# New ranks, fewer q loads and row-wise v tails in a pooled-attention and gated-convolution kernel

## The chip, the core and the metric

The kernel runs on one core of a Trainium2 chip. A core has a matrix engine (TensorE, PE in the profile, with its weight loads as PEld), a vector engine (VectorE, DVE), an activation engine (ScalarE, ACT), a general engine (GpSimd, POOL) and a small engine that here only issues transfers (SyncE, SP). Each engine runs its own instructions in the order in which they were written; semaphores order the engines against each other. Transfers run on 16 DMA engines. The metric is the time of one execution on the device in microseconds (us), as the median of several runs.

## The reference

Eight batches, eight heads, 576 positions, head size 64. Keys and values are averaged over groups of 8 positions, so 576 queries see 72 keys in each head. The attention output, 576 x 512 per batch, goes through a gated feed-forward part:

```
k_p = k.reshape(B, H, 72, 8, D).mean(axis=3);  v_p likewise
attn = softmax(q @ k_p^T / sqrt(D))            # 576 x 72 in each head
x = (attn @ v_p), heads side by side           # 576 x 512 in each batch
h = relu(x @ w_in)                             # 576 x 1024
conv = sum over 3 taps of conv_w[k] * h shifted by k - 1
out = (h * sigmoid(conv)) @ w_out              # 576 x 512
```

All inputs and the output are float32; the kernel computes in bf16 and accumulates in float32.

## The kernel before

**Work by batch.** k, v and q are loaded batch by batch by transfers issued from POOL, which turn float32 into bf16 on the way. Each batch has two buffers in turn (`k_b`, `v_b`, `q_b`, `q2`, `qT`, `attnT`, `xT`, `hT`). VectorE sums 8 neighbours of k (steps kp1, kp2 and ksum, L590, L597 and L607) and of v (vp1, vp2, va, L639), TensorE transposes the sums of k (kT, L620), and these are copied into `kz` (L627). The sums of v are multiplied by a mask into block form (`vblk`, L643 and L648).

v is cut into tiles of 128 rows (L462) and a fifth tile, the tail. The tail holds, for each of four pairs of heads, 32 rows around the 16 that the other tiles lack. One transfer brings all 128 rows (L467); the mask drops what is not wanted.

q comes in two ways. For batches 0 to 4 a transfer of 64 rows and one of 8 (L419) fill `q_b`, a copy regroups it (qg, L427), TensorE transposes it (qT, L673), and copies bring it to `qT` (qTe, L679). For batches 5 to 7 five transfers (L407) bring q by rows of positions, and five crossbar transposes issued from SP (qD, L661) turn it into `qT`, one for each 128 positions. In those batches the attention output is transposed in the same way (xD, L757); in the others by TensorE and a copy (xt and xte, L764 and L770).

Then come the scores (sc, L702 and L704, five steps to a batch; in batches 5 to 7 each reads all five tiles of `qT`), their exponentials on ScalarE (L710), the product with `vblk` (av, L727 and L731), the normalization on VectorE (rc and nm, L740 and L744), the transposes, and the first product (mm1, L784 in batch 0, L807 in the others, eight steps of eight matmuls) with its relu on ScalarE (L813). The convolution is done for a few feature blocks on TensorE (L930, with diagonal weights that POOL builds at L559), for the others by two scalings (cp, L853 on ScalarE or L855 on VectorE) and two sums (L862, L872). The gate follows (L880 or L937 on ScalarE, L908 and L918 on VectorE). The second product (mm2, L961) is done for pairs of batches, in nine tiles of 128 rows; a copy (oe, L984) and a store from SP (st, L989) end it.

**Order.** The program does not write its steps in the order of this list. Each step is first added to a planner with its engine, a duration, what it reads and writes, and, for transfers, their load on the DMA engines. The planner goes through a model of the engines' time: at each point it takes, for each engine, the steps that could start first, and among those that could start within 0.02 us of each other the one with the lowest rank. The ranks are the list `prio`, one whole number for each step in the order in which steps are added. What the planner picks is the order in which the instructions are written, so on the chip each engine has that order and waits where an input is late. The list `act` names the steps that go to ScalarE where both ScalarE and VectorE could do them (cp, oe, qTe, qg, xte, kz); the others go to VectorE. Where the model shows TensorE idle in the first 60 us, `warm` puts in matmuls of zeros (L383).

The transfers issued from POOL use eight semaphores in turn, so the ninth waits for the first to land. The names below have the batch behind the first point: `ldq5.2` is the third load of q of batch 5, `mm2.1.0.0` the first tile of pair 1 in the second product.

Of the kernel before, what the change touches and what calls it, by code (L numbers as in the profile page):

```python
# [61 lines left out]
    "act": (  # L62
# [38 lines left out]


TINY = 1e-20


class Op:
    __slots__ = ("i", "name", "eng", "dur", "lat", "deps", "prio", "fn", "take", "give", "dma", "done", "users", "after", "kind", "unit", "mode")


class Planner:  # L110

# [973 lines left out]
```

## Time and profile before

| | |
|---|---|
| median of 3 runs | 213.72 us (212.86 to 215.43) |
| the profiled execution itself | 213.99 us |
| its span, first to last instruction | 212.3 us |
| busy PE, DVE, ACT, POOL | 196.0, 171.6, 163.6, 57.5 us |
| mean granted TensorE clock | 0.980 |
| read from HBM, written | 33.57 MB, 9.44 MB |

Busy times are those of the span. The page of the profile gives them by engine and in slices of the span; other views group instructions by line, list them in order of time, follow the chain of work that ended last, or name who waited for whom. A row in order of time has its start and its duration in us, the engine, the line, what is written and read, the number of instructions put together, and in brackets the idle time of the engine just before it with what ended that time. In a row that groups instructions by line, behind "x" and their number stand busy us and mean ns of one, then the idle time before them.

### The profile page before, as it was taken

The page shows a single profiled execution, that of the slowest core. Times are in us where ns is not written, and L with a number is a line of the kernel's source. Part 1 is how long each engine was busy: PE and PEld are TensorE (multiplying, and loading weights), DVE is VectorE, ACT ScalarE, POOL GpSimd, SP SyncE. Part 2 cuts the span into 40 slices and gives each one's busy share as a digit, 9 for nine tenths or more (in the row PEclk, how much of TensorE's full clock was granted, in tenths as well). Part 3 has the DMA queues.
Part 4 walks back from the last instruction along what each step waited for, and adds up shares of the span by engine and source line. Part 5 has one row for each costly group of instructions (what it writes and reads, how often), then busy time and mean ns, then how long its engine had stood idle before and what let it go on. Part 6 is the DMA issues. An engine that isn't in the chain of part 4 may idle for free.

```text
span 212.3 us, 4596 instructions
## 1 busy us (share of the span) xinstructions
PE 196.0 (92%) x1776; PEld 133.6 (63%) x1792; DVE 171.6 (81%) x395; ACT 163.6 (77%) x275; POOL 57.5 (27%) x91
## 2 busy tenths in 40 slices
PE   8999988989999959993799999999999999999993
PEld 8988665857576627761376668655755864675541
DVE  3578499999999778999079999997999999478620
ACT  2025599999999947994479999999998995998512
POOL 7993598443241357334400000000000000000000
PEclk9999999999999999999589999999999999999998
DMA  4999999999999999999999117424523503600434
GB/s 67 186 191 201 175 204 194 185 203 180 196 167 244 235 181 148 157 116 152 181 178 126 76 69 139 106 57 131 148 49 114 148 0 84 208 21 0 170 131 148
DMA packets 52282, 30.08 MB, mean 142 GB/s; under 512 B 33356, under 2 KB 47268, under 8 KB 52260
## 3 DMA queue, kind: packets, MB, share of 16 engines
q0 software_dynamic: 32336, 16.79, 67.9%
q1 hardware_dynamic: 19924, 12.99, 24.8%
q8 instruction: 14, 0.23, 0.5%
q14 instruction: 8, 0.07, 0.1%
HBM read 33.57 MB, written 9.44 MB: 203 GB/s over the span
## 4 chain that ended last, share of the span: by engine, by line
PE 52%; DMA 28%; DVE 7%; POOL 5%; SPq 4%; issue 2%; ACT 0%; ACTq 0%; DVEq 0%; POOLq 0%
PE psfB L961 22%; PE psfA L807 20%; DMA k_b<-in_k_dram 8%; DMA q_b<-in_q_dram 8%; DMA v_b<-in_v_dram 7%; DMA qT<-q 5%; SPq L661 4%; PE psfA L727 3%; PE psfA L930 2%; PE psfA L702 2%; DVE p L590 1%; PE psfA L731 1%; DVE cv L862 1%; POOL q_b L419 1%; PE psfA L961 1%
## 5 line engine op out<-in xcount | busy, mean ns | idle before, releaser
L961 PE MATMUL psfB<-w_out,gT 128*128 128x512 bf16 (+1 forms) x267 | 63.4, 377 | 0.9 <-issue 0.2
L807 PE MATMUL psfA<-xT,w_in 128*128 128x288 bf16 x448 | 59.3, 289 | 0.5 <-DVE xT L770 0.5
L807 PEld LDWEIGHTS <-w_in 128*128 128x128 bf16 x448 | 43.3, 99 | 13.3 <-DVE xT L770 0.8
L961 PEld LDWEIGHTS <-gT 128*128 128x128 bf16 x290 | 27.3, 98 | 29.1
L813 ACT ACTIVATE hT<-psfA 128x576 bf16<-128x576 f32 x56 | 35.6, 663 | 3.3 <-PE psfA L807 3.0
L855 DVE TENSOR_SCALAR cv<-hT,cr 128x576 bf16<-128x576 bf16 x72 | 25.2, 370 | 5.7 <-ACT hT L813 3.6
L880 ACT ACTIVATE tg<-cv,cs 128x576 bf16<-128x576 bf16 x37 | 28.3, 789 | 0.3 <-DVE cv L872 0.2
L853 ACT ACTIVATE cv<-hT,cr 128x576 bf16<-128x576 bf16 x36 | 27.4, 783 | 0.2
L744 DVE TENSOR_TENSOR xx<-psfA,rr 128x512 bf16<-128x512 f32 (+1 forms) x40 | 26.6, 677 | 0.2
L918 DVE TENSOR_TENSOR gT<-tg,hT 128x1152 bf16<-128x1152 bf16 x32 | 23.8, 749 | 1.8 <-ACT tg L937 1.7
L710 ACT ACTIVATE attnT<-psfA 128x576 bf16<-128x576 f32 x40 | 24.7, 656 | 0.7 <-PE psfA L702 0.4
L984 ACT COPY osb<-psfB 128x512 f32<-128x512 f32 x25 | 14.6, 589 | 9.4 <-PE psfB L961 9.3
L862 DVE TENSOR_TENSOR cv<-cv,hT 128x1152 bf16<-128x1152 bf16 (+1 forms) x31 | 20.7, 671 | 1.1 <-ACT cv L853 1.0
L872 DVE TENSOR_TENSOR cv<-cv 128x1152 bf16<-128x1152 bf16 (+1 forms) x31 | 20.6, 668 | 1.0 <-ACT cv L853 0.4
L383 PEld LDWEIGHTS <-zero 128*128 128x128 bf16 x261 | 17.0, 107 | 2.2 <-DVE zero L485 1.1
L702 PE MATMUL psfA<-qT,kz 128*128 128x64 bf16 (+1 forms) x63 | 12.7, 289 | 5.4 <-DMA qT<-q 4.9
L407 POOL DMA_DIRECT2D q<-in_q_dram x15 | 12.7, 848 | 15.4 <-PE psbA L673 3.8
L727 PE MATMUL psfA<-vblk,attnT 128*128 128x130 bf16 (+1 forms) x160 | 15.8, 222 | 0.0
L679 ACT COPY qT<-psbB 128x792 bf16<-128x792 bf16 (+2 forms) x8 | 6.3, 808 | 12.3 <-PE psbB L673 12.3
L908 DVE TENSOR_SCALAR tg<-tg 128x1152 bf16<-128x1152 bf16 x22 | 10.0, 456 | 5.5 <-ACT tg L937 5.3
L383 PE MATMUL pswA<-zero 128*128 128x128 bf16 x175 | 12.7, 243 | 1.1 <-DVE zero L485 1.1
L880 ACT ACTIVATE tg<-cv,cn 128x576 bf16<-128x576 bf16 x17 | 12.5, 774 | 1.3 <-DVE cv L872 1.3
(87 smaller groups left out, 259.6 us busy)
## 6 DMA issues: line engine op xcount, KB each, us to landing
out_dram<-osb SPq DMA_DIRECT2D x14, 512.0 KB, 3.1
k_b<-in_k_dram POOLq DMA_DIRECT2D x8, 512.0 KB, 14.9
v_b<-in_v_dram POOLq DMA_DIRECT2D x7, 512.0 KB, 15.0
q_b<-in_q_dram POOLq DMA_DIRECT2D x5, 512.0 KB, 15.6
out_dram<-osb SPq DMA_DIRECT2D x7, 256.0 KB, 2.3
q<-in_q_dram POOLq DMA_DIRECT2D x12, 128.0 KB, 13.8
v_b<-in_v_dram POOLq DMA_DIRECT2D x8, 128.0 KB, 13.9
w_in<-in_moe_w_in_dram POOLq DMA_DIRECT2D x1, 1024.0 KB, 14.2
```

Source lines behind the costliest of these rows:

```text
L383: nc.tensor.matmul(out=t, lhsT=zero[:, 0:P], rhs=zero[:, 0:P], start=True, stop=True)
L710: nc.scalar.activation(out=attnT[m][:, t, :], in_=slot(key).rearrange("p i x -> p (i x)")[:, 0:S], func=ACT.Exp, scale=1.0 / 64.0)
L727: nc.tensor.matmul(out=a[0:n, g, c * w:(c + 2) * w], lhsT=attnT[m][:, s, u0:u0 + n], rhs=vblk[m][:, 2 * s:2 * s + 2, :].rearrange("p x d - ...
L744: nc.vector.tensor_tensor(out=xx[i3][0:n].rearrange("p (g h e) -> p g h e", g=2, h=4), in0=av_view()[:, :, :, 0:D], in1=rr[i3][0:n].rearra ...
L807: nc.tensor.matmul(out=t[:, i, 0:HC], lhsT=w_in[:, c, f * P:(f + 1) * P], rhs=xT[m][:, c, i * HC:(i + 1) * HC], start=(c == 0), stop=(c == ...
L813: nc.scalar.activation(out=h_(b)[:, f, hs(b), 2:S + 2].rearrange("p (i x) -> p i x", i=2), in_=slot(key)[:, :, 0:HC], func=ACT.Relu)
L853: nc.scalar.activation(out=cv[y][:, kk // 2, z0:z1, :], in_=src, func=ACT.Copy, scale=sc)
L855: nc.vector.tensor_scalar(out=cv[y][:, kk // 2, z0:z1, :], in0=src, scalar1=sc, scalar2=None, op0=OP.mult)
L862: nc.vector.tensor_tensor(out=cv[y][:, 0, 0:n, :], in0=cv[y][:, 0, 0:n, :], in1=h_at(2), op=OP.add)
L880: nc.scalar.activation(out=tg[i3][:, zs[z0]:zs[z0] + z1 - z0, :], in_=cv[y][:, 0, z0:z1, :], func=ACT.Tanh if half else ACT.Sigmoid, scale ...
L918: nc.vector.tensor_tensor(out=o_, in0=tg[i3], in1=h2, op=OP.mult)
L961: nc.tensor.matmul(out=a[:, 0, j0:j1], lhsT=g[:, c, t * P:(t + 1) * P], rhs=w_out[:, c, j0:j1], start=(c == 0), stop=(c == n_fb - 1), skip ...
```

## The change

- The list of ranks is replaced by another, and so is the list of steps on ScalarE.
- The tail of v in batch 0 comes in four transfers of 16 rows, just the rows that are wanted. The other rows of the tail tile are cleared once by VectorE, in both buffers; the other batches keep the transfer of 128 rows, which now also stands behind that clearing.
- q of batches 1 to 4 comes in one transfer of 72 rows instead of one of 64 and one of 8. Batch 0 keeps two.
- The planner's model is another: four groups of DMA engines instead of one ring for each issuing engine, a transfer on 16, 12, 8 or 4 of the engines, at most eight transfers from POOL on their way, other durations for steps on POOL, SP and for some small steps on VectorE. The model is not in the program that runs; it only sets the order.
- The number of zero matmuls in a gap of the first 6 us is counted at 0.107 us each instead of 0.058.

Which batches use crossbar transposes is the same before and after.

```diff
     "prio": (
-        "3 14 5 19 15 8 22 4 20 1 31 10 16 72 0 13 23 37 17 25 86 100 58 172 115 179 76 108 "
...
+        "7 17 8 43 28 19 67 48 20 63 30 29 33 60 37 22 42 62 35 41 81 49 57 146 166 102 77 135 "
...
     "act": (
-        "qTe.0.2 xte.0.0 xte.0.1 qTe.1.0 qTe.1.1 xte.1.0 xte.1.1 xte.1.2 cp0.0.0 cp2.0.2 cp0.0.7 cp2.0.7 "
...
+        "kz.0.0 kz.0.1 qTe.0.2 xte.0.0 xte.0.1 xte.0.2 xte.0.3 kz.1.1 qTe.1.0 qTe.1.1 xte.1.0 xte.1.1 "
...
+    "vt": [1, 0, 0, 0, 0, 0, 0, 0],
+    "qs": [1, 0, 0, 0, 0, 0, 0, 0],
...
-    DMA_GAP = 0.7
+    DMA_GAP = 1.5
...
+                    if e == "POOL" and o.dma is not None and len(lanes) >= 8:
+                        s = max(s, lanes[-8] + 0.28)
...
-                own, other = ring[e], ring["SP" if e == "POOL" else "POOL"]
-                t0 = max(own[0], s + d + self.DMA_GAP)
-                both = min(n, max(0.0, (other[0] - t0) / other[1]))
...
+                w = range(o.width)
+                for z in w:
+                    ring[z] = max(ring[z], s + d + self.DMA_GAP) + n * each
...
-    def warm(gap, x):
-        n = min(int((gap + (0.15 if gap > 0.4 else -0.1)) / 0.058), 100)
+    def warm(gap, x, f0):
+        cold = max(0.0, min(gap, 6.0 - f0))
+        hot = gap - cold
+        n = int(max(0.0, cold - 0.1) / 0.107) + (min(int((hot + (0.15 if hot > 0.4 else -0.1)) / 0.058), 100) if hot > 0.12 else 0)
...
-        for x, (r0, r1) in enumerate(((0, 64), (64, PR))):
+        for x, (r0, r1) in enumerate(((0, 64), (64, PR)) if PARAMS["qs"][b] else ((0, PR),)):
...
+            if PARAMS["vt"][b]:
+                for c in range(4):
+                    def fn(e, e0=e0, d=d, op=op, c=c):
+                        nc.gpsimd.dma_start(out=v_b[m][32 * c + 16:32 * c + 32, 4, d], in_=src[P:P + 16, c, e0], **op)
...
+            else:
+                def fn(e, e0=e0, d=d, op=op):
+                    nc.gpsimd.dma_start(out=v_b[m][:, 4, d], in_=src[P - 16:P + 16, :, e0].rearrange("y c e -> c y e"), **op)
...
+            def fn2(e, m=m):
+                nc.vector.memset(v_b[m][:, 4, :], 0.0)
+            pl.add(f"zvt{m}", "DVE", 0.38, fn2, writes=[("vz", m)], prio=-66 + 35 * m)
...
-                pl.add(f"qD.{b}.{t}", "SP", 0.9, fn, reads=[("qn", b % NQ, t)], writes=[("qT", m, t)], free=[("qA", m)],
-                       prio=pr[0] + 0.01 * t, dma=(1, 0.8), lat=1.6)
+                pl.add(f"qD.{b}.{t}", "SP", 1.27, fn, reads=[("qn", b % NQ, t)], writes=[("qT", m, t)], free=[("qA", m)],
+                       prio=pr[0] + 0.01 * t, dma=(1, 0.5), lat=0.1)
```

For the steps that the prediction names, the ranks in the two lists, read off by their place, are these (before, after):

| step | before | after |
|---|---|---|
| first k sum of batch 0 (kp1.0.0) | 27 | 24 |
| convolution weights on VectorE (cw) | 4 | 48 |
| mask (mask0); first 64 rows of q0 (ldq0.0) | 13; 18 | 22; 14 |
| v of batch 0: two large loads | 28, 32 | 15, 21 |
| w_in (ldwi0) | 33 | 31 |
| q of batch 5 (ldq5.0 to ldq5.4) | 363 to 386 | 379 to 463 |
| k of batch 6 (ldk6.t, ldk6.0) | 350, 356 | 471, 480 |
| first k sum of batch 5 (kp1.5.0) | 422 | 470 |
| transposes of q of batch 5 (qD.5.0 to qD.5.4) | 472, 487, 502, 477, 485 | 535, 510, 474, 554, 486 |
| last store of pair 0 (st.0.7) | 542 | 541 |
| last transposes of batch 3's output (xt.3.4) | 558 | 545 |
| first product of batch 3 (mm1.3.0 to mm1.3.7) | 571 to 618 | 539 to 579 |
| second product of pair 1, tiles 0 to 2 | 612, 629, 644 | 601, 615, 623 |
| scores of batch 5, lowest rank | 555 | 636 |

More of the change, by code (lines that the diff above doesn't have):

```diff
@@ L106 @@
 class Op:
-    __slots__ = ("i", "name", "eng", "dur", "lat", "deps", "prio", "fn", "take", "give", "dma", "done", "users", "after", "kind", "unit", "mode")
+    __slots__ = ("i", "name", "eng", "dur", "lat", "deps", "prio", "fn", "take", "give", "dma", "width", "done", "users", "after", "kind", "unit", "mode")
 class Planner:
@@ L139, in add @@
         o.lat = lat
-        o.fn, o.prio, o.take, o.give, o.dma = fn, prio + self.shift.get(name, 0.0), take, give, dma
+        o.fn, o.prio, o.take, o.give, o.dma = fn, prio + self.shift.get(name, 0.0), take, give, dma and dma[:2]
+        o.width = dma[2] if dma and len(dma) > 2 else 4
         deps = set()
@@ L186, in order @@
         self.gaps = {}
-        ring = {"POOL": [0.0, 1.0], "SP": [0.0, 1.0]}
+        ring = [0.0] * 4
+        lanes = []
         busy = {}
@@ L257, in order @@
                 n, each = o.dma
-                own, other = ring[e], ring["SP" if e == "POOL" else "POOL"]
-                t0 = max(own[0], s + d + self.DMA_GAP)
-                both = min(n, max(0.0, (other[0] - t0) / other[1]))
-                own[0] = t0 + n * each + both * other[1]
-                own[1] = each
-                if both:
-                    other[0] += both * each
-                o.done = own[0] + (self.DMA_LAT if o.lat is None else o.lat)
+                w = range(o.width)
+                for z in w:
+                    ring[z] = max(ring[z], s + d + self.DMA_GAP) + n * each
+                o.done = max(ring[z] for z in w) + (self.DMA_LAT if o.lat is None else o.lat)
             else:
                 o.done = s + d + (self.LAT[e] if o.lat is None else o.lat) + self.SEM
+            if e == "POOL" and o.dma is not None:
+                lanes.append(o.done)
             if o.give is not None:
@@ L407, in fn @@
                     nc.gpsimd.dma_start(out=q_rows(b % NQ)[0:n, t].rearrange("p (h d) -> p h d", d=D), in_=q[b, :, P * t:P * t + n].rearrange("h p d -> p h d"))
-                pl.add(f"ldq{b}.{t}", "POOL", 1.0, fn, writes=[("qn", b % NQ, t)], free=[("q", b % NQ, h) for h in range(H)] + [("qt", b % NQ)],
-                       prio=prio + 0.01 * t, dma=packets(n * H, 256))
+                pl.add(f"ldq{b}.{t}", "POOL", 0.88, fn, writes=[("qn", b % NQ, t)], free=[("q", b % NQ, h) for h in range(H)] + [("qt", b % NQ)],
+                       prio=prio + 0.01 * t, dma=packets(n * H, 132))
             return
@@ L416, in load_q @@
             return
[L417 removed]
+        for x, (r0, r1) in enumerate(((0, 64), (64, PR)) if PARAMS["qs"][b] else ((0, PR),)):
             def fn(e, r0=r0, r1=r1):
                 nc.gpsimd.dma_start(out=q_b[b % NQ][r0:r1].rearrange("p h i d -> p h (i d)"), in_=rows_q(b)[r0:r1])
[L420 removed]
+            pl.add(f"ldq{b}.{x}", "POOL", 0.8 - 0.2 * x, fn, writes=[("ql", b % NQ, x)] + ([] if PARAMS["qs"][b] else [("ql", b % NQ, 1)]), prio=prio, dma=packets((r1 - r0) * H, 1024, engines=16 if r1 == 64 else 12 if r0 == 0 else 8))
     def regroup(b, pr):
@@ L464, in load_v @@
                 pl.add(f"ldv{b}.{'a' * i}{x}", "POOL", 0.8, fn, reads=keys if i else [], writes=keys, prio=pr, dma=packets(P * (c1 - c0), 1024 // (1 + acc)))
-            def fn(e, e0=e0, d=d, op=op):
-                nc.gpsimd.dma_start(out=v_b[m][:, 4, d], in_=src[P - 16:P + 16, :, e0].rearrange("y c e -> c y e"), **op)
-            pl.add(f"ldv{b}.{'a' * i}t", "POOL", 0.55, fn, reads=[("v", m, 2)] if i else [], writes=[("v", m, 2)], prio=prio + 0.01 + (PARAMS["ld0"][3] if b == 0 else 0),
-                   dma=packets(P, 1024 // (1 + acc)))
+            if PARAMS["vt"][b]:
+                for c in range(4):
+                    def fn(e, e0=e0, d=d, op=op, c=c):
+                        nc.gpsimd.dma_start(out=v_b[m][32 * c + 16:32 * c + 32, 4, d], in_=src[P:P + 16, c, e0], **op)
+                    pl.add(f"ldv{b}.{'a' * i}t{c}", "POOL", 0.5, fn, reads=[("vz", m)] + ([("v", m, 2 + c)] if i else []), writes=[("v", m, 2 + c)],
+                           prio=prio + 0.01 + (PARAMS["ld0"][3] if b == 0 else 0), dma=packets(16, 1024 // (1 + acc)))
+            else:
+                def fn(e, e0=e0, d=d, op=op):
+                    nc.gpsimd.dma_start(out=v_b[m][:, 4, d], in_=src[P - 16:P + 16, :, e0].rearrange("y c e -> c y e"), **op)
+                pl.add(f"ldv{b}.{'a' * i}t", "POOL", 0.7, fn, reads=[("vz", m)] + ([("v", m, 2 + c) for c in range(4)] if i else []), writes=[("v", m, 2 + c) for c in range(4)],
+                       prio=prio + 0.01 + (PARAMS["ld0"][3] if b == 0 else 0), dma=packets(P, 1024 // (1 + acc), engines=4))
     def weights_in(prio):
@@ L523, in fn @@
                                            op0=OP.is_lt, op1=OP.mult)
-        pl.add("cn0", "DVE", 0.12, fn, reads=["cw", "cna"], writes=["cn0"], prio=-44)
+        pl.add("cn0", "DVE", 0.2, fn, reads=["cw", "cna"], writes=["cn0"], prio=-44)
         def fn(e):
@@ L528, in fn @@
                                            op0=OP.mult, op1=OP.add)
-        pl.add("cn1", "DVE", 0.12, fn, reads=["cw", "cn0"], writes=["cn1"], prio=-43)
+        pl.add("cn1", "DVE", 0.2, fn, reads=["cw", "cn0"], writes=["cn1"], prio=-43)
         def fn(e):
@@ L552, in consts @@
             k = "mask" if x < 2 else "mask4"
-            pl.add(f"mask{x + 1}", "POOL", 0.75, fn, reads=[k], writes=[k], prio=-50)
+            pl.add(f"mask{x + 1}", "POOL", 0.47, fn, reads=[k], writes=[k], prio=-50)
         for f in ON:
@@ L633, in attn_v @@
         m = b % 2
-        tail = [("v", m, 2)]
+        tail = [*[("v", m, 2 + c) for c in range(4)]]
         pool8(b, "v", v_b, pr, ((0, 2, (0,), [("v", m, 0)]), (2, 5, (1,), [("v", m, 1)] + tail)) if b == 0 else
```

15 lines of the change are left out of this document (7 added, 8 removed), and 91 rows, old and new, of the table PARAMS.

## The prediction

> **What bounds the kernel now.** I read the page first, for the span and the shares.
>
> ```profile
> span 212.3 us, 4596 instructions
> PE 196.0 (92%) x1776; PEld 133.6 (63%) x1792; DVE 171.6 (81%) x395; ACT 163.6 (77%) x275; POOL 57.5 (27%) x91
> ```
>
> TensorE is busy for 92% of the span, but that mixes stages with different limits. So I asked for busy times by stretch. The columns are the stretch, its length, busy us (and instructions) of PE, PEld, DVE, ACT and POOL, then the granted clock, the DMA share and GB/s.
>
> ```profile
> 0.00:30.00 30.00, 27.62 (x374) 23.61 (x375) 18.82 (x55) 11.52 (x23) 22.25 (x44) 1.00 1.11 169
> 30.00:97.00 67.00, 62.50 (x650) 43.54 (x653) 63.40 (x148) 60.60 (x104) 31.45 (x44) 1.00 1.50 184
> 97.00:109.00 12.00, 7.10 (x44) 3.62 (x42) 5.21 (x12) 5.13 (x10) 3.85 (x5) 0.72 1.49 178
> 109.00:180.00 71.00, 70.37 (x550) 46.42 (x556) 68.16 (x155) 66.74 (x109) 0.00 (x0) 1.00 0.51 98
> ```
>
> Two engines fill the middle together: from 30 to 97 us VectorE is busy 63.40 of 67, from 109 to 180 us 68.16 of 71, and there TensorE 70.37 of 71. The one hole is 97 to 109 us, where TensorE idles 4.90 of 12 us at a granted clock of 0.72 and VectorE idles 6.79. Between 30 and 180 us VectorE has 3.60 + 6.79 + 2.84 = 13.2 us of idle time, half of it in that hole. PE's timeline says what opens it, and the chain that ended last gives durations (start, us, what).
>
> ```profile
> 96.89 0.41 PE L702 MATMUL psfA<-qT,kz 128*128 128x512 bf16 x2
> 101.61 0.61 PE L702 MATMUL psfA<-qT,kz 128*128 128x512 bf16 x1 [4.31 <-DMA qT<-q]
> 102.80 0.21 PE L702 MATMUL psfA<-qT,kz 128*128 128x64 bf16 x1 [0.59 <-DMA qT<-q]
> 102.95 0.39 PE L764 MATMUL psbB<-perm,xx 64*128 64x64 bf16 x4
> ```
>
> ```profile
> 91.97 10.79 DMA qT<-q
> ...
> 103.34 1.56 PE psfA L930 x6
> ...
> 106.20 7.98 PE psfA L807 x56
> ...
> 117.73 1.73 PE psfB L961 x8
> ...
> 148.89 3.92 PE psfA L807 x32
> ...
> 196.72 0.74 PE psfA L930 x6
> ```
>
> The first scores of batch 5 (L702) wait 4.31 + 0.59 us for the crossbar transposes of its q (L661 writes qT); the last of them lands at 91.97 + 10.79 = 102.76 us. TensorE takes its instructions in order, so what stands behind waits along: batch 3's last output transposes (102.95), whose input VectorE finished at 96.25, and then batch 3's whole first product, since before the wait only 128 / 8 = 16 products of L807 had run, those of batches 1 and 2.
>
> ```profile
> 95.58 0.67 DVE L744 TENSOR_TENSOR xx<-psfA,rr 64x512 bf16<-64x512 f32 x1
> ```
>
> ```profile
> 0.00:101.50 101.50, 16.89 (x128) 12.09 (x128) 1.00 1.39 178
> ```
>
> The idle time also costs clock: six matmuls of L930 take 1.56 us right after it and 0.74 later (0.82 lost), and 56 of L807 take 7.98 where the later 32 in 3.92 make it 6.86 (1.12 lost); for the small products between I estimate 0.3 in the same ratio. The stall costs 4.90 + 2.24 = 7.1 us.
>
> **The change part by part.** The sum is made against the profiled execution: 213.99 us, 1.7 of them outside the span. The median of the runs shown is 213.72, so 0.27 comes off at the end.
>
> *Ranks.* The list gives every step a rank, which decides among steps that are ready. In the old list the earliest score of batch 5 has 555, ahead of batch 3's last output transposes (558) and first products (571 to 618), as the trace ran them. In the new one these have 545 and 539 to 579, three tiles of pair 1's second product 601, 615 and 623, and the earliest score of batch 5 has 636. That puts 8 x 3.92 / 4 = 7.8 us of L807 and 3 x 1.73 = 5.2 us of L961 ahead of the scores. TensorE, free at 97.3, would then reach them at 110.3 or later, against qT at 102.76. The q loads of batch 5 also move ahead of batch 6's k (ranks 379 to 463 against 471 and 480; before, 363 to 386 against 350 and 356). The stall goes: -7.1 us. Bounds are 0 (it turns up elsewhere) and -7.1. Late next are the transposes themselves. This is SP's queue, and their issue to landing over the run (min/median/max).
>
> ```profile
> 82.62 15.92 SPq L661 DMA_TRANSPOSE qT<-q  x6
> 98.63 0.54 SPq L989 DMA_DIRECT2D out_dram<-osb  x1
> ```
>
> ```profile
> DMA to landing us min/median/max: 2.3/9.7/13.3
> ```
>
> Five of these six are batch 5's; the store at 98.63 is pair 0's last. The new list puts that store (541) between two transposes of batch 5 (535 and 554), so the last is queued behind a store that waits for its copy. Issued at 99.2 it lands at 108.9 by the median and 112.5 by the longest: a wait of 0 to 2.2 us behind the cover, priced 0 here and kept for the rivals.
>
> *Copies between ScalarE and VectorE.* Counted over both lists, VectorE gets three cp, two oe and three qTe more, and three kz and one xte fewer; ScalarE the reverse.
>
> ```profile
> L855 DVE TENSOR_SCALAR cv<-hT,cr 128x576 bf16<-128x576 bf16 x72 | 25.2, 370 | 5.7 <-ACT hT L813 3.6 <-ACT tg L880 1.6
> ...
> L984 DVE COPY osb<-psfB 128x512 f32<-128x512 f32 x9 | 6.1, 681 | 1.6 <-PE psfB L961 1.5
> ...
> L770 DVE COPY xT<-psbB 128x512 bf16<-128x512 bf16 (+1 forms) x8 | 3.2, 400 | 0.0
> ...
> L627 DVE COPY kz<-psbB 64x288 bf16<-64x288 bf16 x8 | 2.4, 305 | 1.6 <-PE psbB L621 1.4
> ...
> L679 DVE COPY qT<-psbB 128x576 bf16<-128x576 bf16 (+1 forms) x2 | 1.0, 516 | 0.1
> ```
>
> That is 3 x 0.370 + 2 x 0.681 + 3 x 0.516 - 3 x 0.305 - 0.400 = +2.7 us on VectorE. With the hole gone its idle time in the middle shrinks from 13.2 by 7.1 to about 6 us, 4% of the stretch and the same share as late in the kernel (2.84 of 71), so I take all 2.7 as lost; bounds 0 and 2.7. The two new clears of v's rest rows come first, beside 30 - 18.82 = 11.2 us of VectorE's idle time, and cost nothing; without that cover, their own duration.
>
> *Loads.* Only at the start does their order set the end. The first columns are start and us.
>
> ```profile
> 7.27 0.18 DVE L514 TENSOR_SCALAR cw<-psfB 128x24 f32<-128x24 f32 x1 [2.56 <-PE psfB L510]
> ...
> 8.68 0.82 DVE L590 TENSOR_TENSOR p<-k_b 128x1280 bf16<-128x1280 bf16 x1
> ```
>
> Today VectorE stands 2.56 us for the convolution weights and takes up k at 8.68, behind a chain of small steps. In the new list that chain ranks behind k's sums (24 and following against 48), the copies of kz go to ScalarE, and q and v are issued ahead of the mask. I take -1.0 us, bounds 0 and -2.3: above that w_in, now behind the small v loads, is late next. Three loads in a row, issue and then time to landing, show the sizes.
>
> ```profile
> 30.41 0.61 POOL L419 DMA_DIRECT2D q_b<-in_q_dram  x1
> 31.00 0.71 POOL L467 DMA_DIRECT2D v_b<-in_v_dram  x1
> 31.70 0.80 POOL L462 DMA_DIRECT2D v_b<-in_v_dram  x1
> ```
>
> ```profile
> v_b<-in_v_dram POOLq DMA_DIRECT2D x1, 512.0 KB, 14.0
> v_b<-in_v_dram POOLq DMA_DIRECT2D x1, 128.0 KB, 12.2
> q_b<-in_q_dram POOLq DMA_DIRECT2D x1, 64.0 KB, 10.3
> ```
>
> They land at 40.7, 43.2 and 45.7: the 128 KB tail of v holds the queue 2.5 us, as long as the 512 KB beside it. Batch 0's tail becomes four loads of 16 KB: at worst they take the 2.5 us together, at best nothing that shows beside their neighbours. They issue three more instructions on POOL, 0.7 us each, ahead of w_in. Merging q saves four issues of 0.61 us on POOL, busy 31.45 of 67 us, and no bytes; priced 0, bounds 0 and 1.2 us a load (a 64 KB part at the tail's 2.5 us per 128 KB). Fewer filler matmuls at the start carry no work: 0.
>
> By the Trainium skill, "DMA: Bandwidth & Descriptors", section on why a DMA increments its semaphore by 16, a transfer uses the largest number of engines up to 16 that divides its slowest dimension. The tail of v, with 4 there, agrees at 2.5 us for 128 KB; the merged q, with 72 rows, would use 12 engines where 64 rows used 16, which speaks against this part: an estimate by the page is 576 / 128 x 4 / 12 x 2.5 = 3.75 us where the 512 KB took 2.5. The sum would be 210.6.
>
> Sum: 213.99 - 7.1 - 1.0 + 2.7 = 208.6, less 0.27: **208.3 us**.
>
> **The rivals.**
>
> 1. *Everything fits.* VectorE's 2.7 us find room, the start gives 2.3, and one more wait goes, 2.13 us of TensorE at 78.70, where VectorE had stood 2.30 for batch 5's k:
>
> ```profile
> 75.51 0.83 DVE L590 TENSOR_TENSOR p<-k_b 128x1280 bf16<-128x1280 bf16 x1 [2.30 <-DMA k_b<-in_k_dram]
> ```
>
> The new list moves that step from 422 to 470. Against it: VectorE, with 63.40 + 5.21 + 68.16 + 2.7 = 139.5 us of work there, would have 150 - 7.1 - 2.1 = 140.8 us for it. 213.72 - 7.1 - 2.3 - 2.1 = 202.2 us; chance 0.08.
>
> 2. *The wait only moves.* The late transpose behind the store, or the same pattern at batch 6, holds TensorE again. For it: landings of up to 13.3 us. Against it: 13 us of cover. With 5 of the 7.1 back, 213.3 us; chance 0.13.
>
> 3. *Merged q loads are slower.* Four loads each land 1.2 us later, less 2.5 for batch 0's tail, so by batch 5's k the queue is 2.3 us late and the wait of 2.30 for it grows. 208.3 + 2.3 = 210.6 us; chance 0.10. For it: the tail's slow landing. Against it: the queue is long, and a slow load can pass beside the next one. This is the mechanism of the page named above.
>
> 4. *Slower: VectorE becomes the bound.* It works in order, too; if the new order makes it stand for inputs as long as today, the hole's 6.79 us come back as several short waits between 30 and 180 us, and the moved copies come on top: 213.72 + 2.7 = 216.4 us. It decides from the point where VectorE's idle time there, now 13.2 us, falls by less than 2.7. For it: VectorE's 68.16 of 71 us late. Against it: the hole has one cause, and ScalarE gets lighter. Chance 0.19.
>
> **How the numbers follow.** The forecast itself has 0.50. A measurement of this kernel tells about 1% from no change, 2.1 us. Faster: 0.50 + 0.08 + 0.07 of the third rival = 0.65. Same: 0.03 of the third, 0.10 of the second, 0.03 of the fourth = 0.16. Slower: the rest of the second and fourth, 0.03 + 0.16 = 0.19. The range runs from 203.0, just above the first rival, to 217.0, just past the fourth; outside lie some 0.05 below and 0.12 above, for more than one new stall.
>
> **What would show it.** Right: no PE wait on qT above 1 us between 80 and 115 us, the clock at 1.00 until the last stretch, L807 of batch 3 ahead of batch 5's first scores, VectorE's idle time in the middle near 13.2 - 7.1 = 6 us, k's first sum ahead of 8 us. Wrong: another stall over 3 us with the clock lowered, a wait for q or k in batches 1 to 4 longer than today's, or VectorE idle as long as now.

## The result, and the profile after

The changed kernel took 201.6 us (median of 4 executions, 201.34 to 207.61) against 213.62 us for the kernel before (212.86 to 215.43): a ratio of 0.9455, 95% interval 0.938 to 0.9529. It is 12.0 us faster; 208.3 us were forecast, with a range down to 203.0. Some executions of several of these kernels are 4 to 6 us longer than their others; the ratios leave such out, and the profiled execution of the changed kernel, 207.61 us, is one (VectorE waits 2.50 us for a load of v at 129.53 us). Its lines have other numbers: L702 is now L717, L807 is L822, L744 is L759, L855 is L870, L908 is L923, L559 is L571.

The page's first lines, and busy times by stretch (columns as in the prediction):

```profile
span 205.9 us, 4566 instructions
...
PE 194.9 (95%) x1770; PEld 133.0 (65%) x1770; DVE 173.3 (84%) x396; ACT 165.3 (80%) x275; POOL 57.0 (28%) x90
```

```profile
0.00:30.00 30.00, 27.66 (x370) 23.75 (x371) 21.27 (x57) 14.10 (x29) 25.06 (x49) 1.00 1.08 170
30.00:97.00 67.00, 66.21 (x679) 46.58 (x677) 65.64 (x154) 65.68 (x109) 27.15 (x36) 1.00 1.40 179
97.00:109.00 12.00, 12.00 (x94) 7.88 (x93) 12.00 (x29) 11.97 (x21) 4.13 (x5) 1.00 1.89 160
109.00:180.00 71.00, 66.79 (x514) 43.08 (x513) 60.95 (x136) 60.06 (x99) 0.68 (x1) 0.98 0.78 114
```

The hole from 97 to 109 us is filled: TensorE and VectorE are busy for 12.00 of 12 us at full clock, where they had 7.10 and 5.21. But the stretch ahead of it changed as well: from 30 to 97 us TensorE is busy 66.21 of 67 us instead of 62.50, and ScalarE 65.68 instead of 60.60. (Matmuls of zeros count as busy, but there are about as many of them in that stretch: 46 before, 49 after.) PE's timeline at the old hole:

```profile
93.23 0.92 PE L945 MATMUL psfA<-hT,dw 128*128 128x288 bf16 x6
93.99 8.00 PE L822 MATMUL psfA<-xT,w_in 128*128 128x288 bf16 x64
...
108.28 0.41 PE L717 MATMUL psfA<-qT,kz 128*128 128x512 bf16 x2
```

All 64 products of batch 3 run at 93.99, ahead of batch 5's first score at 108.28, which does not wait. From 28 to 190 us these are TensorE's waits (engine, line, what it waited for, us in all, times, the longest):

```profile
PE psfA L822 <- DMA xT<-xx: 2.2, 1, 2.2
PE psfA L742 <- DVE xx L759: 2.0, 1, 2.0
PE psbA L635 <- DVE ksum L622: 0.3, 1, 0.3
PE psbA L688 <- DVE xx L759: 0.2, 1, 0.2
```

The first two stand at 139 and 131 us and belong to the lengthened execution: the profile of run 1 below has neither. What is left of the old waits is 0.5 us.

VectorE's busy time rose by 1.7 us only (171.6 to 173.3). Its groups show why; first the kernel before, then the changed one (busy us and mean ns behind the bar), then ScalarE's table loads in the changed kernel (a sixth stands at its start):

```profile
L908 DVE TENSOR_SCALAR tg<-tg 128x1152 bf16<-128x1152 bf16 x22 | 10.0, 456 | 5.5 <-ACT tg L937 5.3
```

```profile
L870 DVE TENSOR_SCALAR cv<-hT,cr 128x576 bf16<-128x576 bf16 x75 | 26.3, 378 | 5.6 <-ACT hT L828 5.4
...
L923 DVE TENSOR_SCALAR tg<-tg 128x1152 bf16<-128x1152 bf16 (+1 forms) x17 | 6.8, 402 | 0.7 <-ACT tg L895 0.4 <-ACT tg L952 0.3
```

```profile
L895 ACT ACT_TABLE_LOAD x3 | 3.8, 1283 | 0.1
L725 ACT ACT_TABLE_LOAD x2 | 2.6, 1283 | 0.0
```

The three more scalings cost what was counted (75 of L870 instead of 72, 0.38 us each). But the new order gathers the exponentials in blocks, and between blocks the planner changes ScalarE's table, so that 16 more gates are computed as sigmoids (36 instead of 20). ScalarE pays four more loads of 1.28 us for it (the kernel before has two in all, the changed one six); VectorE is spared the step that turns a tanh into a sigmoid: 10.0 us fell to 6.8.

### The profile page after: what moved, and what is told of

Same layout as the page of the kernel before. It is cut to its first block, busy times and chain, and to the rows that moved or that the text cites. A ratio compares the mean times of both kernels' runs of the same rounds, so it can differ in the third digit from the quotient of the medians.

```text
span 205.9 us, 4566 instructions
## 1 busy us (share of the span) xinstructions
PE 194.9 (95%) x1770; PEld 133.0 (65%) x1770; DVE 173.3 (84%) x396; ACT 165.3 (80%) x275; POOL 57.0 (28%) x90
## 4 chain that ended last, share of the span: by engine, by line
PE 38%; DMA 26%; ACT 16%; DVE 12%; issue 3%; POOL 3%; SPq 0%; POOLq 0%; DVEq 0%; ACTq 0%
PE psfB L976 14%; DMA v_b<-in_v_dram 13%; PE psfA L822 12%; DMA q_b<-in_q_dram 6%; DMA qT<-q 6%; ACT tg L895 4%; PE pswA L388 3%; ACT attnT L725 3%; PE psfA L742 2%; ACT hT L828 2%; ACT cv L868 2%; PE psfA L945 2%; DVE p L605 2%; DVE cv L870 1%; DMA xT<-xx 1%
## 5 line engine op out<-in xcount | busy, mean ns | idle before, releaser
L976 PE MATMUL psfB<-w_out,gT 128*128 128x512 bf16 (+1 forms) x282 | 65.4, 378 | 0.0
L822 PE MATMUL psfA<-xT,w_in 128*128 128x288 bf16 x448 | 60.0, 291 | 2.2 <-DMA xT<-xx 2.2
L822 PEld LDWEIGHTS <-w_in 128*128 128x128 bf16 x448 | 43.9, 100 | 16.2 <-DMA xT<-xx 2.4
L870 DVE TENSOR_SCALAR cv<-hT,cr 128x576 bf16<-128x576 bf16 x75 | 26.3, 378 | 5.6 <-ACT hT L828 5.4
L759 DVE TENSOR_TENSOR xx<-psfA,rr 128x512 bf16<-128x512 f32 (+1 forms) x40 | 26.5, 679 | 0.2
L868 ACT ACTIVATE cv<-hT,cr 128x576 bf16<-128x576 bf16 x33 | 25.1, 776 | 0.4 <-DVE cv L887 0.2
L895 ACT ACTIVATE tg<-cv,cn 128x576 bf16<-128x576 bf16 x30 | 22.5, 780 | 0.0
L895 ACT ACTIVATE tg<-cv,cs 128x576 bf16<-128x576 bf16 x24 | 18.2, 772 | 0.2
L388 PEld LDWEIGHTS <-zero 128*128 128x128 bf16 x239 | 16.1, 108 | 2.8 <-DVE zero L497 2.0
L742 PE MATMUL psfA<-vblk,attnT 128*128 128x130 bf16 (+1 forms) x160 | 15.6, 222 | 2.1 <-DVE xx L759 2.0
L742 PEld LDWEIGHTS <-attnT 128*128 128x128 bf16 (+1 forms) x160 | 11.1, 100 | 5.7 <-DVE xx L759 2.9
L388 PE MATMUL pswA<-zero 128*128 128x128 bf16 x150 | 11.5, 249 | 2.0 <-DVE zero L497 2.0
L717 PE MATMUL psfA<-qT,kz 128*128 128x512 bf16 x64 | 12.4, 286 | 0.3
L746 PE MATMUL psfA<-vblk,attnT 128*128 128x130 bf16 (+1 forms) x80 | 11.2, 221 | 0.0
## 6 DMA issues: line engine op xcount, KB each, us to landing
w_out<-in_moe_w_out_dram POOLq DMA_DIRECT2D x2, 512.0 KB, 12.5
```

Source lines behind the costliest of these rows:

```text
L388: nc.tensor.matmul(out=t, lhsT=zero[:, 0:P], rhs=zero[:, 0:P], start=True, stop=True)
L742: nc.tensor.matmul(out=a[0:n, g, c * w:(c + 2) * w], lhsT=attnT[m][:, s, u0:u0 + n], rhs=vblk[m][:, 2 * s:2 * s + 2, :].rearrange("p x d - ...
L759: nc.vector.tensor_tensor(out=xx[i3][0:n].rearrange("p (g h e) -> p g h e", g=2, h=4), in0=av_view()[:, :, :, 0:D], in1=rr[i3][0:n].rearra ...
L822: nc.tensor.matmul(out=t[:, i, 0:HC], lhsT=w_in[:, c, f * P:(f + 1) * P], rhs=xT[m][:, c, i * HC:(i + 1) * HC], start=(c == 0), stop=(c == ...
L868: nc.scalar.activation(out=cv[y][:, kk // 2, z0:z1, :], in_=src, func=ACT.Copy, scale=sc)
L870: nc.vector.tensor_scalar(out=cv[y][:, kk // 2, z0:z1, :], in0=src, scalar1=sc, scalar2=None, op0=OP.mult)
```

## Experiments

Most kernels below have the planner's choices written out: the order as one list of names, the buffers in PSUM, and, from the ninth run on, the function of each gate. So one step can be moved while the rest stays; where a move makes a chosen buffer unavailable, a neighbouring one is taken. Line numbers are shifted by these lists. The runs were made in groups, each group on one chip with the kernel before beside it, which took 213.6 to 215.2 us (medians).

**1. The changed kernel again.** No edit.

> The changed kernel once more, unchanged, for a profile of an execution at its usual time. Theory A (the time went with TensorE's waits): 201.6 us; TensorE idle under 1.5 us between 30 and 97 us, where the kernel before has 67 - 62.50 = 4.50, and no wait over 1 us from 97 to 150 us. Theory B (VectorE's time was saved, its waits being the bound): the same time, but TensorE idle as long as before between 30 and 97 us, and VectorE's idle time from 30 to 180 us lower by some 10 us than the 13.2 of before.

Ratio 0.9546 (0.9464 to 0.9627), 204.27 us beside 214.32. Its span is 202.5 us, and TensorE has one long wait, 2.4 us at 35.38 us, for diagonal weights (dw) that GpSimd builds. Apart from it TensorE idles 0.3 us between 30 and 97 us, where it had idled 4.50. So theory A holds, with a wait that the first profile did not have (runs 14 and 15). This wait matters for what follows: the profiles of runs 4, 7, 8 and 12, which are kernels made from the changed one, do not have it either. As far as one profile of each can say, their fair measure is the changed kernel without it, 201.6 us above or 201.94 us in run 15, and not this run's 204.27.

**2. The kernel before, scores later.** (Order; the other engines keep theirs.)

```diff
 xte.3.3
-sc.5.1
 xt.3.4 xte.3.4
-sc.5.4 exp.5.1
 mm1.3.0
-exp.5.4
 mm1.3.1 mm1.3.3 mm1.3.5 mm1.3.6 mm1.3.4 mm1.3.2
+sc.5.1 exp.5.1
 sc.5.2 exp.5.2
+sc.5.4 exp.5.4
 mm1.3.7
```

> The kernel before, with one thing altered: the first two scores of batch 5 and their exponentials stand behind batch 3's first product. Theory A (the stall is worth its 4.90 us of idle time and 2.24 us of clock, and nothing takes its place): 213.6 - 7.1 = 206.5 us. Rival (the wait only moves, to the scores' new place or to a later batch): 211 to 214 us. Rival (VectorE is the bound behind the stall, its idle time of 6.79 us in the hole comes back as short waits): 209 to 213 us.

Ratio 0.9874 (0.9778 to 0.997), 2.7 us gained by the ratio. The move had a side effect: three gates of batch 2 became sigmoids, with two more table loads, and TensorE waited 2.1 us for an exponential behind one of them. The same with the first sums of batch 5's k later as well (run 3) gave 0.9887 (0.98 to 0.9974), no more. Runs 9 to 11 repeat these moves without the side effect.

**4. The changed kernel, one score early.**

```diff
 kz.5.0
+kz.5.1 sc.5.3 exp.5.3
 mm1.3.3
-kz.5.1
 mm1.3.2
...
 mm1.3.7
...
-sc.5.3
...
-exp.5.3
```

> The changed kernel, with one thing altered: one score of batch 5 (tile 3), its exponential and the copies of kz that it needs stand ahead of batch 3's first product again. Theory A (the place of the scores decides): the score waits for the last transposes of q, landing at about 104.7 us, some 10 us behind its new place at 94 us, of which the products that used to fill this time are held up: slower by 7 us or more, 208.5 to 213 us. Rival (the transfers' order, or the other engines' order, had removed the stall): within 1 us of 201.6 us.

PE's timeline of this kernel, with the idle time before each row in brackets:

```profile
92.78 0.92 PE L1021 MATMUL psfA<-hT,dw 128*128 128x288 bf16 x6
105.20 0.64 PE L793 MATMUL psfA<-qT,kz 128*128 128x512 bf16 x2 [11.50 <-issue]
106.58 5.62 PE L898 MATMUL psfA<-xT,w_in 128*128 128x288 bf16 x31 [0.74 <-ACT attnT L801]
```

Ratio 1.0137 (1.0074 to 1.0199): 1.4% slower than the kernel before, and 13.3 us slower than the changed one of the same group, which had the wait of 2.4 us besides. The wait of 11.50 us stands where the score was put. Its row names no releaser, but the last of batch 5's transposes, issued at 92.69 us, landed 12.3 us later, at 105.0. The clock of the stretch from 97 to 109 us was 0.50. (Seven gates changed their function by the move.) The place of the scores decides over the stall; the order of the transfers had not removed it.

**5. Scores later, and batch 7's sums later on VectorE**, since in run 2 VectorE had waited 6.0 us for batch 7's k and 2.6 for its v.

```diff
 (scores as in run 2)
-kp1.7.0 kp2.7.0 ksum.7 vp1.7.0 vp2.7.0
 nm.4.4
+kp1.7.0 kp2.7.0 ksum.7
...
+vp1.7.0 vp2.7.0
 va.7
```

> The kernel before, with the scores of batch 5 moved as in the run above, and on VectorE also the sums of batch 7's k behind the normalization of batch 4 and those of batch 7's v behind batch 5's first one. Theory C (behind the stall stood a second one: VectorE's early steps for k and v of batch 7, which land at 100 to 116 us; it took the place of the first): the 5.96 + 2.61 us that VectorE waited for them are gone, and with them TensorE's waits of 2.10, 0.76 and 2.89 and the half clock behind the last; 213.6 - 7.1 = 206.5 us. Rival (VectorE is the bound and stands for something else as long): 210 us or more.

209.61 us beside 215.11; ratio 0.9878 (0.975 to 1.0005). VectorE's waits for k and v fell to 1.2 us, TensorE's behind the table loads stayed. With batch 5's sums moved too (run 6) it was 210.34 us, ratio 0.9922 (0.9824 to 1.002). Neither reached the 206.5 or 204.4 us expected.

**7. The changed kernel with the old transfers.**

```diff
-    "vt": [1, 0, 0, 0, 0, 0, 0, 0],
-    "qs": [1, 0, 0, 0, 0, 0, 0, 0],
+    "vt": [0, 0, 0, 0, 0, 0, 0, 0],
+    "qs": [1, 1, 1, 1, 1, 1, 1, 1],
```

> The changed kernel in its own order, with the transfers of before: q of batches 1 to 4 in 64 and 8 rows, the tail of batch 0's v in one transfer of 128 rows. My sum had priced both at nothing: within 1 us of the changed kernel. Rival 3 (the merged q's are slower, as 72 rows would use 12 engines; they landed 4.6 to 5.4 us behind the transfer ahead of them): faster by up to 2.3 us than the changed kernel if q's are on the path, less up to 2.5 if the tail is.

Ratio 0.964 (0.929 to 0.999), executions of 203.54 to 209.30 us: too wide to tell 2 us. Its two best, 203.5 and 205.4, lie on both sides of run 1's 204.3 and above the 201.6 of the first measurement, so the new loads may have gained up to some 2 us, or nothing. In the first profile of the changed kernel the merged loads did land late. Its timeline of GpSimd's issues (start, us), then its view of the transfers with the time from issue to landing:

```profile
17.96 0.78 POOL L467 DMA_DIRECT2D v_b<-in_v_dram  x1
18.77 0.71 POOL L571 TENSOR_SCALAR dw<-ident,cw 128x128 bf16<-128x128 bf16 x2
19.44 0.90 POOL L424 DMA_DIRECT2D q_b<-in_q_dram  x1
20.34 0.77 POOL L447 DMA_DIRECT2D k_b<-in_k_dram  x1
```

```profile
q_b<-in_q_dram POOLq DMA_DIRECT2D x1, 576.0 KB, 15.5
v_b<-in_v_dram POOLq DMA_DIRECT2D x1, 512.0 KB, 12.3
k_b<-in_k_dram POOLq DMA_DIRECT2D x1, 512.0 KB, 16.2
```

v lands at 30.3, q at 34.9, k at 36.5 us. The 72-row q lands 4.6 us behind v, but the 512 KB of k only 1.6 us behind q, so k seems to have passed in part beside q. Together they took 6.2 us, where two 512 KB loads at the prediction's 2.5 would take 5.0. By the rule of the Trainium skill ("DMA: Bandwidth & Descriptors", on why a DMA increments its semaphore by 16) 72 rows go on fewer engines than 64; the trace agrees, as the prediction's estimate by that rule, 3.75 us for q, makes 6.25 with the 2.5. In the profile no step of TensorE behind 28 us waited for these loads.

**8. More work on VectorE.** The changed kernel, behind each of the 16 steps vb:

```diff
+            for _ in range(2):
+                nc.vector.tensor_scalar(out=scr, in0=scr, scalar1=cs[:, 0:1], scalar2=None, op0=OP.mult)
```

> The changed kernel with 32 more scalings of 128x576 on VectorE (two behind each of the 16 steps that put v into block form), 0.37 us each, 11.8 us in all; they read and write a tile that nothing else uses. My sum's step (VectorE's added work counts in full): slower by some 11.8 us. Theory A (TensorE is the bound, VectorE's idle time takes up what it can; from 30 to 180 us it idles 150 - 139.8 = 10.2 us in the changed kernel): slower by 1.6 us (11.8 - 10.2) if every idle moment can be used, and by 3 to 8 us if half of it can.

The page's busy times of this kernel, and behind them those of run 1:

```profile
PE 193.9 (93%) x1754; PEld 132.4 (64%) x1770; DVE 182.3 (88%) x429; ACT 165.7 (80%) x275; POOL 56.7 (27%) x90
```

```profile
PE 193.3 (95%) x1770; PEld 131.6 (65%) x1770; DVE 172.6 (85%) x396; ACT 165.0 (82%) x275; POOL 62.9 (31%) x90
```

VectorE's 9.7 us more (11.8 were expected) made the span 5.7 us longer than that of run 1 (208.2 against 202.5), and 8.3 us longer than that of run 15 (199.9), which like this one has no wait for diagonal weights. So 1.4 us of the 9.7 found room, at most 4.0. Median 209.84 us, ratio 0.9892 (0.977 to 1.0013).

**9 to 11. The moves of runs 2, 5 and 6 with every gate's function kept.** (Edits as there.)

> The kernel before with the scores of batch 5 moved, as in the second run, but every gate keeps the function (tanh or sigmoid) that it has in the kernel before. In the second run three gates of batch 2 had become sigmoids by the move, which put two more table loads of 1.28 us on ScalarE, and TensorE waited 0.64 and 2.10 us for what stood behind them. Theory C (the stall is worth 7.1 us, but VectorE's wait for batch 7's k and v, which land late, takes part of its place): 2 to 4 us under the kernel before. Theory A (nothing takes its place): 7.1 us under it.

> The same with the sums of batch 7's k and v moved back on VectorE as well, gates as before. The run with these moves and the changed gates was 5.5 us under the kernel before; TensorE waited there 1.83 + 0.70 us behind the two table loads. Theory C: 5.5 + 2.5 = 8.0 us under the kernel before, at least 7.1. Rival (the table loads were hidden, and what is left is VectorE's time): 5 to 6 us under it.

> The same with the first sums of batch 5's k behind the normalization of batch 2 as well. Theory C (each of TensorE's waits counts in full): 2.1 us less than the run above, some 10 us under the kernel before and near the changed kernel. Rival (between 30 and 97 us a wait taken away comes back elsewhere, as in the run that had all three moves and the changed gates, which was no faster than the one without the third): within 0.7 us of the run above.

Scores alone: 0.9686 (0.9622 to 0.9751), 6.7 us. With batch 7's sums: 0.9768 (0.9698 to 0.9838), 5.0 us. With batch 5's too: 0.9833 (0.977 to 0.9897), 3.6 us. The 6.7 us are those of two executions of run 9, 206.85 and 207.19 us; the other two took 211.14 and 211.26. In the first two the scores are worth nearly what was predicted for them. Neither further move gained; the two together lost, while what each did alone lies within the noise. In the profile of run 9, of the execution of 211.14 us, these are TensorE's first waits:

```profile
PE psbB L843 <- DVE xx L823: 4.4, 1, 4.4
PE psbA L843 <- DVE xx L823: 0.8, 1, 0.8
PE psfA L886 <- ACT attnT L789: 0.8, 1, 0.8
PE psfA L781 <- ACT attnT L789: 0.7, 1, 0.7
PE psfA L886 <- DVE xT L849: 0.5, 1, 0.5
PE psfA L781 <- DVE kz L706: 0.5, 1, 0.5
```

The 4.4 us go back to VectorE waiting 5.5 us for batch 7's v. So theory C names what lengthened this execution, but moving the sums does not mend it; which step they then delayed I have not settled. The two waits on attnT come from the move itself: the scores now follow one another faster than their exponentials.

**12. The changed kernel with one change of table.** 17 gates are tanh again:

```diff
-gates as sigmoid: 36, in three blocks
+gates as sigmoid: 19, all behind the last exponential
```

> The changed kernel in its own order, but with 17 gates as tanh again that the new order had made sigmoids (the order gathers the exponentials, so that the planner changes ScalarE's function table in between): ScalarE loses 4 table loads of 1.28 us, VectorE gets back the corrections of these gates, 10.0 us in the kernel before against 6.8 in the changed one. Theory D (the 3.2 us that VectorE saves here are what made room for the 2.7 us of copies, and VectorE's work counts as in the run with 9.7 us more on it, 0.6 to 0.8 of it): 2 to 3 us slower than the changed kernel. Theory A (TensorE is the bound, and both are hidden): within 1 us of it.

The page's busy times of this kernel:

```profile
PE 194.0 (94%) x1751; PEld 133.0 (64%) x1767; DVE 175.3 (85%) x402; ACT 160.8 (78%) x271; POOL 65.6 (32%) x90
```

Ratio 0.9537 (0.9489 to 0.9585), 203.85 us. VectorE has 2.7 us more than in run 1 (175.3 against 172.6), as much as the prediction had charged for the copies, and ScalarE 4.2 less. Beside run 1's 0.9546 the time does not seem to move. But run 1 has the wait of 2.4 us for diagonal weights, and this profile has other waits of TensorE:

```profile
PE psfA L901 <- DMA xT<-xx: 2.2, 1, 2.2
PE psfA L821 <- DVE xx L838: 2.2, 3, 0.9
PE psbB L767 <- DVE kz L721: 0.6, 1, 0.6
...
PE psbA L767 <- DVE xx L838: 0.2, 1, 0.2
```

VectorE holds TensorE up for 3.0 us here, against 0.2 in runs 1 and 15. Beside the changed kernel without the other wait (ratios 0.9455 and 0.9399) run 12 is some 2 to 3 us slower, which is what theory D said. It is not settled: this profile is of an execution of 208.19 us, and no execution of 203.8 us, its usual time, was profiled.

**13. The kernel before again.** No edit.

> The kernel before, unchanged, for a second profile on the chip on which the others of this group run. Theory E (the stall before batch 5's scores is in every execution, the wait of 2.13 us behind batch 5's k is not, since the runs with only the scores moved no longer showed it): a wait on qT of 4 to 5 us with the half clock behind it, the three waits of 0.79, 0.5 and 0.5 us between 35 and 50 us, and no wait above 1 us from 50 to 95 us. Rival: the 2.13 us stand there again.

214.7 us, ratio 1.0007 (0.9961 to 1.0054), span 212.5. TensorE's waits, then two rows of its timeline, the chain's row that ends with the last transpose, and the busy times of the stretch behind it:

```profile
PE psfA L702 <- DMA qT<-q: 7.9, 2, 5.6
PE psbA L764 <- DVE xx L744: 0.8, 1, 0.8
PE psfA L727 <- DVE xx L744: 0.7, 1, 0.7
PE psfA L807 <- DVE xT L770: 0.5, 1, 0.5
PE psfA L930 <- DVE qT L679: 0.5, 1, 0.5
PE psfA L702 <- DVE kz L627: 0.5, 1, 0.5
```

```profile
100.48 0.61 PE L702 MATMUL psfA<-qT,kz 128*128 128x512 bf16 x1 [5.65 <-DMA qT<-q]
103.35 0.21 PE L702 MATMUL psfA<-qT,kz 128*128 128x64 bf16 x1 [2.26 <-DMA qT<-q]
```

```profile
88.39 14.93 DMA qT<-q
```

```profile
103.50:108.00 4.50, 4.50 (x30) 2.43 (x30) 1.84 (x3) 3.26 (x6) 0.00 (x0) 0.50 1.34 194
```

Theory E holds, but for the size of the stall. The 2.13 us behind batch 5's k are gone, and the stall is longer than expected: 5.65 + 2.26 us, and 4.50 us of work at half clock, which is 2.25 lost. 10.2 us in all, where the first profile had 7.1. Five waits of 0.5 to 0.8 us remain, 2.9 together.

**14 and 15. The changed kernel beside it, and with its diagonal weights earlier.** Run 14 has no edit; run 15 on GpSimd:

```diff
+dw4.1 dw4.2 dw2.0 dw5.1 dw6.2 dw2.1
 ldwo0
-dw4.1 dw4.2 dw2.0 dw5.1
 ldv2.t
-dw6.2 dw2.1
 ldwo1
```

> The changed kernel, unchanged, beside it. Theory F (its 201.6 us of the first measurement and 204.3 of the second differ by TensorE's wait for the diagonal weights that GpSimd builds, 2.42 us; four of these scalings took 3.17 us in one profile and 9.25 in the other): either no such wait and 201.3 to 202 us, or one of 2 to 3 us and 203.5 to 204.5 us. Rival: other than that, with waits elsewhere.

> The changed kernel with one thing altered on GpSimd: six scalings that build diagonal weights stand ahead of the first load of w_out, which waits 2.9 us for a semaphore, instead of behind it. Theory F: they are done before the convolution of batch 0 needs them, and the time is 201.3 to 202 us on every chip, 2 to 2.7 us less than the unchanged one where that has the wait. Rival (the wait goes to another place, as VectorE is dense there): as the unchanged one.

204.58 us, ratio 0.9518 (0.9431 to 0.9606), and 201.94 us, ratio 0.9399 (0.9319 to 0.9478); the executions, 203.18 to 205.21 and 201.04 to 202.36, do not overlap. This version beats both kernels measured beside it. TensorE's longest wait in run 14, then GpSimd's timelines in run 1 and in run 15:

```profile
PE psfA L945 <- POOL dw L571: 2.4, 1, 2.4
```

```profile
26.08 9.25 POOL L571 TENSOR_SCALAR dw<-ident,cw 128x128 bf16<-128x128 bf16 x4
```

```profile
21.50 2.80 POOL L650 TENSOR_SCALAR dw<-ident,cw 128x128 bf16<-128x128 bf16 x8
```

Four scalings that take 9.25 us behind the wait for w_out's semaphore become part of eight that take 2.80 us ahead of it. Theory F holds: this wait, with the clock that it costs (0.97 from 30 to 97 us in run 1), is the difference between 204.3 and 201.6 us. In run 15 TensorE waits 0.65 us in all between 28 and 190 us (0.27, 0.20 and 0.18), and the span is 199.9.

**16. The kernel before, scores later, three small waits taken away.** On VectorE:

```diff
-vp2.1.0
 kz.1.0 kz.1.1
+vp2.1.0
...
-g.0.0 g.0.4
 rc.1.0 rc.1.1 nm.1.0 rc.1.2 nm.1.1
+g.0.0 g.0.4
...
-vp1.2.0
 xte.1.3 xte.1.4
+vp1.2.0
```

> The kernel before with the scores of batch 5 moved and the gates kept (6.5 us less than before in its undisturbed runs), and three more moves on VectorE, each putting what TensorE waits for ahead of what nothing waits for: batch 1's kz ahead of the second sum of its v, the first two normalizations of batch 1 ahead of two gate products, two copies to xT ahead of the first sum of batch 2's v. Theory G (the rest of the gain of the new order is a row of such small waits, each counting in full): the 0.49, 0.79 and 0.52 us go, 1.8 us less than with the scores alone, some 8.3 us under the kernel before. Rival (TensorE only waits for the next thing): within 0.7 us of the scores alone.

Ratio 0.9716 (0.9545 to 0.9886), which shows no gain over run 9. The waits for kz, xx and xT there shrank, and others came: 1.1 us for the next batch's kz and 0.8 for a later xx. Theory G finds no support: in this one profile the single moves passed such a wait on.

**17 and 18. Empty work on TensorE** in the kernel before and in that of run 15:

```diff
+            if o.name == "mm2.0.4.0":
+                warm(2.0, ...)
```

> The kernel before with 37 matmuls of zeros ahead of the fifth tile of pair 0's second product (at about 66 us), which carry no work and take TensorE 37 x 0.058 = 2.1 us. Theory H (the stall's end is fixed by the transfers: q's transposes land at 102.8 and 103.3 us in the two profiles of this kernel, whether TensorE had waited 2.13 us at 78.70 or not; so what TensorE loses ahead of the stall lies in its shadow, and the stall alone, measured in one execution, is no measure of what goes with it): within 0.7 us of the kernel before, the stall 2 us shorter. Rival (each wait counts in full): 2.1 us slower.

> The changed kernel with the diagonal weights built earlier (201.9 us), and the same 37 matmuls of zeros ahead of the same tile (at about 72 us). Theory H (no stall is left to hide them): 2.1 us slower, 203.5 to 204.5 us. Rival (TensorE is not the bound there, VectorE or ScalarE is): within 0.7 us of 201.9 us.

PE's timeline in the kernel before with the zeros:

```profile
103.44 0.61 PE L702 MATMUL psfA<-qT,kz 128*128 128x512 bf16 x1 [5.95 <-DMA qT<-q]
106.37 0.21 PE L702 MATMUL psfA<-qT,kz 128*128 128x64 bf16 x1 [2.33 <-DMA qT<-q]
```

Ratio 1.0028 (0.9899 to 1.0158), which does not tell 0 from 2 us; but the stall is no shorter than in run 13, it ends 3.0 us later (106.37 for 103.35). By this one profile theory H falls for the kernel before: the stall moved along with the work ahead of it. The version of run 15 took 203.66 us with the zeros, 0.9517 (0.9448 to 0.9587): 1.7 us more by the medians, 2.5 by the ratios, about the 2.1 put in. At that place TensorE sets the pace.

## Why the prediction was wrong

*The place and the mechanism were right.* The stall stood before batch 5's scores, the new ranks took it away, and it comes back by their place alone (run 4). The late transposes behind the store were no trouble: the scores come at 108.28 us and do not wait.

*The first step that failed is "so I take all 2.7 as lost".* The sum counted what the new lists put on VectorE and not what they take off it. The new order of the exponentials made 16 more gates sigmoids and gave VectorE 3.2 us back; I had not looked for that. VectorE's busy time rose by 1.0 us in run 1 and 1.7 in the first profile, and TensorE's waits for VectorE in the middle were only 0.2 us in run 1 and, ahead of 130 us, 0.5 in the first profile. So most of the surcharge did not arise, and the rest held TensorE up little. The price itself was not far off: where the gates' gift is taken away (run 12), the time is some 2 to 3 us above that of the changed kernel without the wait for diagonal weights, and 9.7 us on VectorE cost 5.7 to 8.3 (run 8).

*The second, and larger, is that TensorE's other idle time was priced at nothing.* Between 30 and 97 us it was 67 - 62.50 = 4.50 us, and I had taken only its largest piece, 2.13 us, and only as a rival. It fell to 0.79, which is 3.7 us. Together the two steps make 6.4 of the 6.7 us between 208.3 and 201.6. From the first pair of profiles the gain is 7.1 + 3.7 + 0.6 (the first product at 22.24 instead of 22.85) = 11.4 of the 12.0 us measured.

*The size of the stall was taken from one execution.* "The stall costs 4.90 + 2.24 = 7.1 us"; the second profile has 10.2. In the first one a load was late at 78.70, TensorE came later to the scores (97.30 instead of 94.84 us), and the transposes landed 10.79 us after their issue instead of 14.93. From the pair on one chip, runs 13 and 15, the gain is 10.2 for the stall and 2.9 - 0.65 for the small waits, 12.5 of the 12.6 us between 212.5 and 199.9. Both sums add rows of traces and are no tests. Moving the scores alone gained 6.7 us at best; the profile of run 9 has new waits behind them.

*The rivals.* The first, "everything fits" (202.2 us, chance 0.08), came nearest in time, but not by its terms: it had 2.3 us for the start, and the 2.13 us at 78.70 that it took away are not in the second profile of the kernel before. Part of that nearness is luck.

VectorE's timeline at the start of the changed kernel:

```profile
8.25 0.18 DVE L526 TENSOR_SCALAR cw<-psfB 128x24 f32<-128x24 f32 x1 [1.02 <-PE psfB L522]
...
8.79 0.84 DVE L605 TENSOR_TENSOR p<-k_b 128x1280 bf16<-128x1280 bf16 x1 [0.16 <-DMA k_b<-in_k_dram]
```

*The start* was near in size, 0.6 us for 1.0, but not by the way given: the convolution weights still come first on VectorE, and k's first sum is at 8.79 us, not ahead of 8. Nor is the size firm: in run 13 the kernel before has its first product at 22.38 us. *The loads* priced at nothing cost nothing that could be measured. *VectorE's idle time* from 30 to 180 us was to fall to 6 us; in run 1 it is 150 - 139.8 = 10.2, but in run 15, without the wait for diagonal weights, 150 - 142.4 = 7.6, which is near the forecast.

What stays open is which of the many moves in the order of batches 1 to 4 removes the small waits. Three that looked like it showed no gain (run 16), nor did those of runs 10 and 11, and run 7 leaves up to 2 us to the new loads; shown is only that the changed kernel as a whole leaves TensorE next to none (0.65 us in run 15).

## What to carry to other kernels

Before a stall is priced, take a second profile of the same kernel: its length here was 7.1 us in one execution and 10.2 in another, at the same total time. Then add up all the idle time of the engine that sets the pace, small pieces too, since a new order can take all of them at once though no single move tried here did. For a second busy engine, count all that the new order puts on it and all that it takes off, and measure what added work costs there by adding a known amount. And before two runs are compared, look whether both profiles have the same waits: the one for diagonal weights hid 2 to 3 us in runs 8 and 12.

## What the runs showed of the hardware

The 15 scalings of 128x128 that GpSimd does took 0.56 us each in the first profile of the changed kernel, 0.99 in the second and 0.43 when they stood earlier; four of them took 3.17 us or 9.25. The slow ones ran while VectorE was busy without a gap, the fast eight at 21.5 us while it did little. This agrees with the Trainium skill ("SBUF — State Buffer", section "SBUF: two separate sides"): GpSimd and some of VectorE's forms share a pair of ports as an exclusive lock, and the one that comes second is blocked for the other's whole instruction. But the four that took 3.17 us ran beside an equally dense VectorE, in the same order, and in run 4, on the chip of run 1, they took 5.31; why they differ so stays open.

The crossbar transposes landed up to 14.93 us after their issue while loads were on their way. And a gate that changes from tanh to sigmoid moves work between engines: 16 of them took 3.2 us from VectorE for 5.1 us of table loads on ScalarE.
